# SwiGLU operands of the second half of the tokens by way of DRAM, down products kept back, and a plan with more time for low parts

## The chip, the core and the metric

The kernel runs on one core of a Trainium2 chip. The metric is the device time of one execution in microseconds (us). TensorE (PE) multiplies; its weight loads have a track of their own (PEld). VectorE (DVE), ScalarE (ACT) and GpSimd (POOL) work element by element, and the queue of SyncE (SP) issues nearly all transfers (DMA).

## The reference

One transformer block on 2048 tokens of width 512, batch 1, all float32, with a modulation that is computed from a condition vector `c`:

```python
mod = (_silu(c) @ w_mod).reshape(c.shape[0], 6, 1, -1)
sa, ca, ga, sb, cb, gb = (mod[:, 0], ..., mod[:, 5])
h = _layernorm(x, axis=-1) * (1 + ca) + sa
x = x + ga * attention(h)          # 32 heads of 16, causal window of 256, output product wo
h = _layernorm(x, axis=-1) * (1 + cb) + sb
gate = h @ w1; up = h @ w3         # 512 -> 1792 each
x = x + gb * ((_silu(gate) * up) @ w2)
```

## The kernel before

**Precision.** Every operand of a product is kept as two tiles: a high part, which is the value rounded to the type that TensorE reads at full rate, and a low part, which is the value less the high part. A product is three matmuls: high by high, high by low and low by high. The high part is made by ACT, the low part by POOL or DVE. `split` (lines 914 to 922) does both for tiles that come from DRAM.

**Stages.** Attention fills the first half of the time; its order is written by hand. Behind it come the output product with the second residual (`o_proj`, line 1068 for the matmuls), and then the feed-forward part, which the change is about. The last part of attention and all that follows are ordered by a planner, `Sched.deal`: each operation has an engine, a planned duration, a key (the smaller, the earlier it is chosen among those that can start) and the tiles that it reads and writes. It simulates the engines and writes the instructions out in the order that it finds; each engine's queue then runs in that order, and every wait is for the data itself. `CAPS` says how many PSUM banks each use may hold. The dictionary `K` holds the keys' offsets and the engines chosen for some operations; `fl` is the spacing of the keys from one block of features to the next. Keys and planned times only set an order: nothing on the chip waits for a clock.

**Feed-forward.** The tokens are worked through in two halves of 1024, and a half in seven blocks `p` of 256 features of gate and up. In a block, `ffn` makes gate and up (`up(0)`, `up(1)`) by a scheme of seven products for a two by two block matrix instead of eight. The right-hand operands are the seven operands `B11, T2, T3, T1, B21, T4, B22` (in the order of their use, each two tiles of 512 tokens for the two slices of the width, high and low), made from the four quarters of the modulated, normalised and transposed rows: width halves by token halves. T1 to T4 are differences: T1 = h12 - h11, T2 = h22 - T1, T3 = h22 - h12, T4 = h21 - T2. Each product is two slices of the width by three matmuls of 128 by 128 by 512 (line 1253). The block ends with eight down products (line 1344), six matmuls each, whose results DVE adds to the residual rows `x1` (line 1349). The downs of a block are issued during the up products of the next.

**Operands of a half.** `ln2(half)` makes the tiles of B and T: ACT normalises eight row tiles (line 1177), TensorE turns each by four transposes into a bank (line 1191), ACT modulates while copying out (line 1195), POOL and DVE take the differences (line 1208), ACT makes the high parts (line 1214) and POOL or DVE the low parts (line 1216). `ln2(0)` runs behind the output product, `ln2(1)` at the boundary of the halves. There is one set of these tiles, and two sets of weight tiles, `WT[0]` and `WT[1]`, taken in turn: block `p` of either half uses set `p % 2`, so that the last block of the first half (p = 6) and the first of the second (p = 0) use the same set. The normalised rows of `ln2` lie in eight buffers, `wqr`, `e0` to `e2` and `g0` to `g3`; the last four are also the gates of a block.

**Weights.** `load_w` loads a block's weights from DRAM (line 1126) and splits them (lines 918 and 920), `load_w2` the two rows of tiles of w2 (line 1159), for which there is one buffer. During the first half, `late_job` still prepares sums of weights for later blocks: it loads to `e0` or `e1`, works on POOL and stores (line 1156). The output goes out from line 1353.

**After the up products** of a block: gate by ACT (Silu, line 1276), times up by DVE (line 1280), high part by ACT (line 1323), low part by DVE (line 1326), and then the down products can start. The parts of all blocks lie in the same eight buffers (`wq00` to `qk2`).

Of the kernel before, what the change touches and what calls it, by code (L numbers as in the profile page):

```python
# [18 lines left out]
P = 128  # L19
# [34 lines left out]
CAPS = dict(up=3, dn=5)  # L54


def act(n):
    return 0.053 + 0.00083 * n
# [38 lines left out]
class Sched:  # L97
# [35 lines left out]
    def deal(self):  # L133
# [17 lines left out]
        while left:  # L151
# [87 lines left out]
def us(t):  # L239
# [15 lines left out]
K = dict(wo=0.254, x1=5.304, xb=-4.504, xl=0.319, os=0.261, ol=(-6.755, 2.066, 21.413, 4.993),  # L255
         pl=(9.985, -12.537, 2.397, 130.962), pe=(5.247, -7.512, 44.055, 93.798), o=(2.808, 8.131,
         12.136, 6.541), n=(3, 1, 1, 1), w0=0.022, l2=1.493, f=3.77, fl=36.492, by=((('POOL',
         'POOL'), ('POOL', 'DVE'), ('DVE', 'DVE'), ('DVE', 'DVE')), (('POOL', 'POOL'), ('DVE',
         'POOL'), ('DVE', 'POOL'), ('POOL', 'DVE')), (('POOL', 'POOL'), ('POOL', 'DVE'), ('POOL',
         'POOL'), ('DVE', 'POOL')), (('POOL', 'DVE'), ('DVE', 'DVE'), ('POOL', 'DVE'), ('POOL',  # L260
         'POOL'))), w=0.195, dn=0.541, ds=0.105, l3=-19.958)
@with_exitstack
def block_kernel(ctx: ExitStack, tc: tile.TileContext, x, wqk, wv, wo, w13, w2, c, wmod, out):
# [28 lines left out]
    wsum = drm.tile([NP, 2, 2, P, 4 * P], F32, name="wsum")  # L292

# [621 lines left out]
    def split(hi, lo, key, kh, kl, kr=None, raw=None, n=512):  # L915

        src = raw or (lambda: lo().bitcast(F32))
        sch.op("ACT", lambda: nc.scalar.activation(hi(), src(), AF.Copy), act(n), key,  # L918
               [kr or kl], [kh])
        sch.op("POOL", lambda: nc.gpsimd.tensor_tensor(out=lo(), in0=src(), in1=hi().bitcast(F32),  # L920
                                                       op=ALU.subtract), 0.06 + 0.0024 * n, key,
               [kr or kl, kh], [kl])
# [105 lines left out]
    def on_eng(e):  # L1028
        return nc.vector if e == "DVE" else nc.gpsimd

# [58 lines left out]
    def fp_open(key):  # L1089
        def go():  # L1090
# [12 lines left out]
            f"g{m}" for m in range(4)] + [f"e{m}" for m in range(3)]  # L1103
# [14 lines left out]
    def load_w(half, p, key):  # L1118
        s = p % 2
# [38 lines left out]
    def load_w2(p, key):  # L1158
        dma(lambda: nc.sync.dma_start(W2[1].bitcast(F32), w2g[p]), key,
            [("w2g", p, f) for f in range(2)], [("w2", f, 1) for f in range(2)], 512)  # L1160
# [72 lines left out]

    downs = []

    def ffn(half, p, key, fl):
        s = p % 2
        gk = {}

# [77 lines left out]
        for t in range(2):  # L1317
            for f in range(2):
                o = 2 * f + t
                hn, ln = (("wq00", "wq10"), ("wq01", "wq11"), ("qkr", "qk0"), ("qk1", "qk2"))[2 * t + f]  # L1320
# [3 lines left out]
                    fresh(hk + (0,), hn, F32R), tiles[gk[o]], AF.Copy), act(512) + 0.1,  # L1324
                       k1 + 0.5 * (2 * t + f), [f"g{o}"], [hn])
                sch.op("DVE", lambda o=o, hk=hk, ln=ln: nc.vector.tensor_tensor(  # L1326
                    out=fresh(hk + (1,), ln, F32R), in0=tiles[gk[o]],
                    in1=tiles[hk + (0,)].bitcast(F32), op=ALU.subtract), dve(512) + 0.1,
                       k1 + 0.5 * (2 * t + f), [f"g{o}", hn], [ln])

        def down():
            load_w2(p, key + fl * (K["dn"] + K["ds"] * 8))
            for t in range(2):
                for i in range(4):
                    at = 8 * half + 4 * t + i
                    bk = Bank("dn")
                    kk = key + fl * (1 + K["dn"] + K["ds"] * (4 * t + i))

                    def go(t=t, i=i, bk=bk):
                        m = 0  # L1340
                        for f in range(2):
                            hk = hs[f, t][0]
                            for h, y in PARTS:
                                nc.tensor.matmul(ps(bk), tiles[hk + (h,)][:, i * P:(i + 1) * P],  # L1344
                                                 W2[y][:, f], start=(m == 0), stop=(m == 5))
# [47 lines left out]
    for half in range(2):  # L1393
        for p in range(NP):
# [17 lines left out]
            if n:  # L1412
                add_(k - 0.05, lambda half=half, p=p, k=k: load_w(half, p, k - fl + K["w"]), ("w", n))
# [57 lines left out]
```

## Time and profile before

| | us |
|---|---|
| three runs | 1082.97, 1086.78, 1091.92; median 1086.78 |
| the profiled execution | 1086.46 |
| its span, first to last instruction | 1084.7 |
| PE busy / share of the span | 1005.1 / 93% |
| DVE / ACT / POOL busy | 728.2 / 562.9 / 587.6 |
| mean granted clock of TensorE | 0.975 |

Attention with its output product reaches to about 620 us, the first half of the feed-forward part from about 600 to 826, the second half from 850 to the end. Views that the text uses: the page, whose slices are fortieths of the span in tenths of busy time; windows, which give each engine's busy time and number of instructions in a stretch, with TensorE's granted clock (1.00 is full) and the transfers; the timeline, one row for neighbouring instructions of one kind with start, length and, in brackets, the idle time before and what ended it; groups by line, with count, total and mean; and waits, with total, number and longest. A matmul's row is longer than the time it takes from the next, because matmuls overlap; the distance between starts is what one costs.

### The profile page before, as it was taken

Reading aid. Unit: us, or ns where it says so; the run is one execution under the profiler, and the core shown is the slowest. Engines: PE = TensorE matmul, PEld = TensorE weight load, DVE = VectorE, ACT = ScalarE, POOL = GpSimd, SP = SyncE. Lnnn points to the kernel's source line nnn. Section 1 sums busy time; section 2 is a strip of 40 time slices with the busy share of each in tenths; the row PEclk is TensorE's granted clock in tenths of the full one; section 3 lists DMA queues with packets and bytes.
Section 4 is the critical chain, followed back from the end, with each engine's and each line's share of the span. In section 5 each row is a group of like instructions: output and inputs, shape, how many; then the busy total and the mean of one; then the engine's idle time right before and its main releaser. Section 6 shows DMA issues by size and latency. Waiting matters only on the chain.

```text
span 1084.7 us, 17131 instructions
## 1 busy us (share of the span) xinstructions
PE 1005.1 (93%) x5432; PEld 721.3 (66%) x5432; DVE 728.2 (67%) x1887; ACT 562.9 (52%) x1252; POOL 587.6 (54%) x727
## 2 busy tenths in 40 slices
PE   5999999999999999999897899999997999999997
PEld 3677666565656555565465677877776777778785
DVE  7685677676767676777635866566766876655665
ACT  2435667676666666667557644333535533333221
POOL 7432655665565656565548476878745444444211
PEclk9999999999999999999899999999998999999998
DMA  7621555544464545445666153655322321222002
GB/s 280 175 50 43 154 121 126 125 107 118 114 163 116 130 114 139 118 117 135 190 204 214 56 169 117 207 182 164 132 70 91 102 78 55 88 88 79 30 1 97
DMA packets 74510, 131.68 MB, mean 121 GB/s; under 512 B 8626, under 2 KB 21426, under 8 KB 74292
## 3 DMA queue, kind: packets, MB, share of 16 engines
q1 hardware_dynamic: 73700, 129.54, 42.0%
q10 hardware_dynamic: 720, 1.05, 0.3%
q8 instruction: 43, 0.70, 0.3%
q14 instruction: 47, 0.39, 0.1%
HBM read 79.96 MB, written 30.41 MB: 102 GB/s over the span
## 4 chain that ended last, share of the span: by engine, by line
PE 50%; DVE 13%; POOL 13%; DMA 12%; issue 7%; ACT 3%; SPq 1%; POOLq 0%; DVEq 0%; ACTq 0%
PE mx L1253 8%; PE st L1253 7%; DMA ring<-qk 7%; POOL qk L419 5%; PE st L1344 5%; PE mx L1344 4%; PE mx L456 4%; PE pj L401 4%; PE st L621 4%; PE po L683 4%; PE st L707 3%; PE pj L1344 3%; DVE g L1280 3%; POOL pt L735 2%; DVE wq L1326 2%
## 5 line engine op out<-in xcount | busy, mean ns | idle before, releaser
L463 DVE CUSTOM_DVE_ANT_0 junk<-mx,mskq 128x384 bf16<-128x384 f32 (+2 forms) x512 | 267.6, 528 | 89.6 <-PE mx L456 86.5
L456 PE MATMUL mx<-ring 96*128 96x384 f32 (+2 forms) x512 | 178.0, 361 | 28.5 <-DMA ring<-qk 18.9
L707 PE MATMUL st<-ring 100*128 100x384 f32 (+2 forms) x512 | 159.4, 356 | 3.1 <-ACT pt L728 2.0
L401 PE MATMUL pj<-hT,wq 128*128 128x512 f32 x384 | 155.9, 421 | 0.4 <-DVE hT L321 0.4
L456 PEld LDWEIGHTS mx<-ring 96*128 96x128 f32 x512 | 95.7, 192 | 90.5 <-DVE mt L463 40.8
L920 POOL TENSOR_TENSOR w<-w,w 128x512 fp32r<-128x512 f32 (+2 forms) x60 | 114.4, 1918 | 63.3 <-ACT w L918 63.3
L735 POOL TENSOR_SCALAR_AFFINE_SELECT pt<-pt 128x256 f32<-128x256 f32 x224 | 90.0, 406 | 82.2 <-ACT pt L728 74.4
L728 ACT ACTIVATE pt<-st 128x256 f32<-128x256 f32 x224 | 84.9, 395 | 53.7 <-DVE st L725 52.7
L683 PE MATMUL po<-pt,vS 128*17 128x384 f32 (+2 forms) x1408 | 111.8, 397 | 0.1
L707 PEld LDWEIGHTS st<-ring 100*128 100x128 f32 x512 | 98.5, 195 | 16.1 <-ACT pt L728 5.6
L419 POOL TENSOR_TENSOR qk<-qkr,qk 128x512 fp32r<-128x512 f32 x64 | 82.2, 1284 | 41.7 <-ACT qkr L407 39.2
L719 ACT ACTIVATE pt<-st 128x384 f32<-128x384 f32 (+2 forms) x172 | 77.2, 456 | 37.1 <-PE st L710 32.3
L725 DVE COPY_PREDICATED st<-later,st 128x128 f32<-128x128 uint8 x224 | 65.5, 293 | 45.6 <-PE st L707 45.3
L1296 POOL TENSOR_TENSOR t<-t,t 128x512 f32<-128x512 f32 x28 | 36.2, 1293 | 106.1 <-DVE t L1284 98.7
L401 PEld LDWEIGHTS pj<-hT,wq 128*128 128x128 f32 x384 | 73.4, 193 | 25.7 <-issue 18.4
L1253 PE MATMUL mx<-b,w 128*128 128x512 f32 x312 | 78.5, 393 | 2.6 <-ACT t L1287 2.6
L1253 PE MATMUL st<-b,w 128*128 128x512 f32 x288 | 72.1, 392 | 0.0
L1253 PEld LDWEIGHTS mx<-b,w 128*128 128x128 f32 x312 | 58.8, 189 | 15.8 <-ACT t L1287 3.0
L1276 ACT ACTIVATE g<-t 128x512 f32<-128x512 f32 x42 | 25.9, 629 | 83.2 <-POOL t L1296 60.0
L1253 PEld LDWEIGHTS st<-b,w 128*128 128x128 f32 x288 | 54.4, 189 | 11.8
L1284 DVE TENSOR_TENSOR t<-st,t 128x512 f32<-128x512 f32 x51 | 35.0, 686 | 37.2 <-PE st L1253 34.3
L1280 DVE TENSOR_TENSOR g<-t,g 128x512 f32<-128x512 f32 x42 | 56.6, 1349 | 2.9 <-POOL t L1296 1.0
(229 smaller groups left out, 2053.2 us busy)
## 6 DMA issues: line engine op xcount, KB each, us to landing
ring<-qk SPq DMA_DIRECT2D x192, 128.0 KB
o_dr<-os SPq DMA_DIRECT2D x32, 256.0 KB
w<-wsum SPq DMA_DIRECT2D x16, 512.0 KB
w<-w2g SPq DMA_DIRECT2D x14, 512.0 KB
jb<-in_w SPq DMA_DIRECT2D x24, 256.0 KB
w<-wraw SPq DMA_DIRECT2D x16, 384.0 KB
wraw<-in_w SPq DMA_DIRECT2D x7, 768.0 KB
vS<-in_wmod SPq DMA_DIRECT2D x20, 256.0 KB
```

The lines of the kernel that those rows point to most:

```text
L401: nc.tensor.matmul(v["ps"], WQ[g][w][:, n // 3], hTp(i, n // 3, b * BT, BT), start=(n == 0), stop=(n == 3 * KC - 1))
L419: nc.gpsimd.tensor_tensor(out=v[n], in0=v["raw"], in1=v[1].bitcast(F32), op=ALU.subtract)
L456: nc.tensor.matmul(v[i][:, :n], queries(NS, a, gq, 1), keys(NS, hh, a, k0, gq + 1 - k0), start=True, stop=True)
L463: nc.vector.tensor_tensor_reduce(out=junk[:, :n], in0=v[i][:, :n], in1=mskq[:, 3 * P - n:], scale=1.0, scalar=-3e38, op0=ALU.add, op1=ALU. ...
L683: nc.tensor.matmul(po[32 * i:32 * i + DH + 1, qb * P:(qb + nq) * P], vS[:, kb, 4 * g + i], pts[i // 2][:, i % 2, c0:c0 + nq], start=first, ...
L707: nc.tensor.matmul(ps[:, :nq], keys(NM, hh, a, kb, 1), queries(NM, a, kb, nq), start=True, stop=not plus)
L728: nc.scalar.activation(held[u, j, a][:, hh, :2], v[j, a, hh][:, :2], AF.Exp, scale=SCALE)
L735: nc.gpsimd.affine_select(out=pt[:, :, 2 * m], in_=pt[:, :, 0], **w)
L920: sch.op("POOL", lambda: nc.gpsimd.tensor_tensor(out=lo(), in0=src(), in1=hi().bitcast(F32), op=ALU.subtract), 0.06 + 0.0024 * n, key, [kr ...
L1253: nc.tensor.matmul(ps(bk), WT[s, n][w][:, col], BB[t, k][r], start=start and c == 0, stop=stop and c == 5, skip_group_check=True)
L1280: sch.op("DVE", lambda: nc.vector.tensor_mul(tiles[gk[o]], src(), tiles[gk[o]]), dve(512) + 0.1, k1, reads + [gn], [gn])
L1344: nc.tensor.matmul(ps(bk), tiles[hk + (h,)][:, i * P:(i + 1) * P], W2[y][:, f], start=(m == 0), stop=(m == 5))
```

## The change

- **Operands by way of DRAM.** `ln2(1)` is gone. In the first half, `half_rows` normalises, turns and modulates the rows of the second half's tokens (at blocks 1 and 2) and stores the eight tiles to `h_dr`, all by way of one tile `e3`; `half_sums` (at blocks 3 and 4) loads them again, takes the eight differences on POOL and stores them to `t_dr`. At the boundary `load_b` loads 14 tiles straight into the places of the low parts and calls `split` on each; `K["be"]` says which engine makes each low part.
- **Weight tiles** alternate across the boundary: the set is `(half * NP + p) % 2`.
- **The last blocks.** The down products of the block before the last get `K["de"]` on their key. The last block has other buffers for four of its parts, and its w2 goes to the free first tile of weight set 0.
- **The plan.** The result of ACT, DVE or POOL that TensorE reads counts as ready 0.8 us later (`PEM`); up products may hold five banks instead of three, and the transposes of `half_rows` one; the planned time of the low parts of the gated features goes to 1.0 us; all numbers in `K` are others, among them those for the last part of attention and the output product.

```diff
-CAPS = dict(up=3, dn=5)
+CAPS = dict(tp=1, up=5, dn=5)
...
             for u in o.users:
-                u.est = max(u.est, s + (o.lat if u.eng != o.eng or o.kb else o.occ))
+                m = PEM if u.eng == "PE" and o.eng in ("ACT", "DVE", "POOL") else 0.0
+                u.est = max(u.est, s + (o.lat + m if u.eng != o.eng or o.kb else o.occ))
...
+PEM = 0.8
...
-K = dict(wo=0.254, x1=5.304, xb=-4.504, xl=0.319, os=0.261, ol=(-6.755, 2.066, 21.413, 4.993),
-         pl=(9.985, -12.537, 2.397, 130.962), pe=(5.247, -7.512, 44.055, 93.798), o=(2.808, 8.131,
-         12.136, 6.541), n=(3, 1, 1, 1), w0=0.022, l2=1.493, f=3.77, fl=36.492, by=((('POOL',
...
-         'POOL'))), w=0.195, dn=0.541, ds=0.105, l3=-19.958)
+K = dict(be=(('DVE', 'POOL'), ('DVE', 'POOL'), ('DVE', 'POOL'), ('DVE', 'POOL'), ('DVE', 'POOL'),
+         ('POOL', 'POOL'), ('DVE', 'POOL')), hr=9.016, de=18.699, wo=0.403, x1=3.432, xb=-3.473,
+         xl=0.573, os=0.346, ol=(-6.127, -2.69, 14.829, 4.08), pl=(10.986, -0.476, -6.236,
+         31.344), pe=(5.042, -12.993, 12.016, 237.531), o=(3.133, 8.773, 14.919, 2.52), n=(1, 1,
+         1, 1), w0=0.71, l2=1.803, f=4.032, fl=41.71, by=((('POOL', 'POOL'), ('DVE', 'DVE'),
...
+         dn=0.504, ds=0.172, l3=-112.914)
...
+    h_dr = drm.tile([KC, 2, P, BT], F32, name="h_dr")
+    t_dr = drm.tile([4, 2, P, BT], F32, name="t_dr")
...
-        s = p % 2
+        s = (half * NP + p) % 2
...
+    def w2_of(last, part, f):
+        return WT[0, 0][part][:, f * D:f * D + D] if last else W2[part][:, f]
+
+    def w2_keys(last, f, q):
+        return [("w", 0, 0, q, s) for s in range(2)] if last else [("w2", f, q)]
+
+    def load_w2(p, last, key):
+        def go():
+            to = (WT[0, 0][1][:, :2 * D].rearrange("p (f c) -> p f c", f=2) if last else W2[1])
+            nc.sync.dma_start(to.bitcast(F32), w2g[p])
+        dma(go, key, [("w2g", p, f) for f in range(2)],
+            [y for f in range(2) for y in w2_keys(last, f, 1)][:2], 512)
         for f in range(2):
-            split(lambda f=f: W2[0][:, f], lambda f=f: W2[1][:, f], key + 4 + 1.3 * f,
-                  ("w2", f, 0), ("w2", f, 1))
+            split(lambda f=f: w2_of(last, 0, f), lambda f=f: w2_of(last, 1, f), key + 4 + 1.3 * f,
+                  w2_keys(last, f, 0), w2_keys(last, f, 1))
...
+    def half_rows(t, at_):
+
+        names = ("wqr", "e2", "t4", "t5")
+        b = 2 + t
+        ln_rstd(b, at_)
+        for i in range(4):
+            def go(i=i):
+                h = fresh(("xn", 1, 4 * t + i), names[i], F32, (P, D), "a1" if i == 0 else "fp")
+                nc.scalar.activation(h, x1(4 * b + i), AF.Identity, bias=LN[b][3][:, i:i + 1],
+                                     scale=LN[b][2][:, i:i + 1])
+            o = sch.op("ACT", go, act(512) + 0.1, at_, [("x1", 4 * b + i), "rsB%d" % b, "nbB%d" % b], [names[i]])
+            o.est = at_
+        for kk in range(4):
+            bk = Bank("tp")
+
+            def turn(kk=kk, bk=bk):
+                for i in range(4):
+                    nc.tensor.transpose(ps(bk)[:, i * P:(i + 1) * P],
+                                        tiles["xn", 1, 4 * t + i][:, kk * P:(kk + 1) * P], ident)
+
+            def mod(kk=kk, bk=bk):
+                nc.scalar.activation(fresh(("h", kk, t), "e3", F32, (P, BT), "fp"), ps(bk), AF.Identity,
+                                     bias=modc[:, 2, kk:kk + 1], scale=modc[:, 3, kk:kk + 1])
+            sch.op("PE", turn, 4 * TURN, at_, names, [bk])
+            sch.op("ACT", mod, act(512) + 0.15, at_, [bk], ["e3"])
+            dma(lambda kk=kk: nc.sync.dma_start(h_dr[kk, t], tiles["h", kk, t]), at_ + 0.5 * kk, ["e3"],
+                [("h_dr", kk, t)])
+
+    def half_sums(k, at_):
+
+        def load(kk, t, name):
+            y = ("hs", k, kk, t)
+            dma(lambda: nc.sync.dma_start(fresh(y, name, F32, (P, BT), "fp"), h_dr[kk, t]), at_,
+                [("h_dr", kk, t)], [name], hold=True)
+            return y, name
+
+        def sub(m, o, a, b):
+            sch.op("POOL", lambda: nc.gpsimd.tensor_tensor(out=tiles[o[0]], in0=tiles[a[0]], in1=tiles[b[0]],
+                                                           op=ALU.subtract), 1.29, at_, [a[1], b[1]], [o[1]])
+            dma(lambda: nc.sync.dma_start(t_dr[m - T1, k], tiles[o[0]]), at_, [o[1]], [("t_dr", m, k)])
+        h11 = load(k, 0, "t4")
+        h12 = load(k, 1, "t5")
+        h22 = load(k + 2, 1, "e2")
+        sub(T1, h11, h12, h11)
+        sub(T3, h12, h22, h12)
+        h21 = load(k + 2, 0, "e3")
+
+        sub(T2, h22, h22, h11)
+        sub(T4, h21, h21, h22)
+
+    def load_b(key):
+
+        for n, m in enumerate((B11, T2, T3, T1, B21, T4, B22)):
+            for k in range(2):
+                if m in (B11, B21, B22):
+                    src = h_dr[k if m == B11 else k + 2, 1 if m == B22 else 0]
+                    dep = ("h_dr", k if m == B11 else k + 2, 1 if m == B22 else 0)
+                else:
+                    src, dep = t_dr[m - T1, k], ("t_dr", m, k)
+                dma(lambda m=m, k=k, src=src: nc.sync.dma_start(BB[m, k][1].bitcast(F32), src),
+                    key + 0.1 * n, [dep], [("b", m, k, 1)])
+                split(lambda m=m, k=k: BB[m, k][0], lambda m=m, k=k: BB[m, k][1], key + 0.1 * n,
+                      ("b", m, k, 0), ("b", m, k, 1), eng=K["be"][n][k])
+
...
-                hn, ln = (("wq00", "wq10"), ("wq01", "wq11"), ("qkr", "qk0"), ("qk1", "qk2"))[2 * t + f]
+                hn, ln = (("wq00", "wq10"), ("wq01", "wq11"), ("qkr", "qk0"), ("qk1", "qk2"),
+                          ("e0", "e1"), ("e2", "wqr"))[2 * t + f + (2 if last and t else 0)]
                 hk = ("hh", half, p, f, t)
                 hs[f, t] = hk, hn, ln
                 sch.op("ACT", lambda o=o, hk=hk, hn=hn: nc.scalar.activation(
-                    fresh(hk + (0,), hn, F32R), tiles[gk[o]], AF.Copy), act(512) + 0.1,
+                    fresh(hk + (0,), hn, F32R, (P, BT), "fp" if hn[0] == "e" else "a1"), tiles[gk[o]], AF.Copy), act(512) + 0.1,
                        k1 + 0.5 * (2 * t + f), [f"g{o}"], [hn])
                 sch.op("DVE", lambda o=o, hk=hk, ln=ln: nc.vector.tensor_tensor(
-                    out=fresh(hk + (1,), ln, F32R), in0=tiles[gk[o]],
-                    in1=tiles[hk + (0,)].bitcast(F32), op=ALU.subtract), dve(512) + 0.1,
+                    out=fresh(hk + (1,), ln, F32R, (P, BT), "fp" if ln[0] == "e" else "a1"), in0=tiles[gk[o]],
+                    in1=tiles[hk + (0,)].bitcast(F32), op=ALU.subtract), 1.0,
...
-                    kk = key + fl * (1 + K["dn"] + K["ds"] * (4 * t + i))
+                    kk = key + fl * (1 + K["dn"] + K["ds"] * (4 * t + i)) + (
+                        K["de"] if half and p == NP - 2 else 0.0)
...
+            if half == 0 and p in (1, 2):
+                add_(k - 0.3, lambda p=p: half_rows(p - 1, te + K["hr"] + 20 * (p - 1)), ("rows", p - 1))
+            if half == 0 and p in (3, 4):
+                add_(k - 0.3, lambda p=p: half_sums(p - 3, te + K["hr"] + 40 + 15 * (p - 3)), ("sums", p - 3))
...
-                add_(k + 0.01, lambda k=k: ln2(1, k + K["l3"]), ("ln2", 1))
+                add_(k + 0.01, lambda k=k: load_b(k + K["l3"]), ("ln2", 1))
```

More of the change, by code (lines that the diff above doesn't have):

```diff
@@ L913, in fresh, with on_eng, split, src @@
         return tiles[key]
[L915 to L922, printed above, removed]
+    def on_eng(e):
+        return nc.vector if e == "DVE" else nc.gpsimd
+    def split(hi, lo, key, kh, kl, n=512, eng="POOL"):
+        def src():
+            return lo().bitcast(F32)
+        kh, kl = (y if isinstance(y, list) else [y] for y in (kh, kl))
+        sch.op("ACT", lambda: nc.scalar.activation(hi(), src(), AF.Copy), act(n), key, kl, kh)
+        sch.op(eng, lambda: on_eng(eng).tensor_tensor(
+            out=lo(), in0=src(), in1=hi().bitcast(F32), op=ALU.subtract),
+               0.06 + 0.0024 * n if eng == "POOL" else 0.85, key, kl + kh, kl)
     LN = {}
@@ L1234, in block_kernel @@
     downs = []
     def ffn(half, p, key, fl):
-        s = p % 2
+        s = (half * NP + p) % 2
         gk = {}
+        last = half == 1 and p == NP - 1
         def up(n):
```

19 lines of the change are left out of this document (7 added, 12 removed).

## The prediction

> **What bounds the kernel now.** I read the page first, for the engines and the slices, and then one view of windows for the time after attention, because every edit lies there.
>
> ```profile
> span 1084.7 us, 17131 instructions
> PE 1005.1 (93%) x5432; PEld 721.3 (66%) x5432; DVE 728.2 (67%) x1887; ACT 562.9 (52%) x1252; POOL 587.6 (54%) x727
> PE   5999999999999999999897899999997999999997
> ```
>
> TensorE bounds it. From 560 us on, the question is how far each window falls short of a TensorE that never waits and runs at full clock. The columns are window, length, PE busy (x instructions), PEld, DVE, ACT, POOL, granted clock, DMA share and GB/s.
>
> ```profile
> 560.00:600.00 40.00, 33.27 (x147) 25.57 (x145) 21.60 (x41) 27.67 (x50) 30.57 (x20) 0.96 0.63 205
> 600.00:660.00 60.00, 53.41 (x216) 41.65 (x215) 39.24 (x61) 32.16 (x56) 35.13 (x26) 0.94 0.34 111
> 660.00:820.00 160.00, 158.12 (x680) 126.95 (x679) 104.77 (x122) 62.05 (x96) 110.10 (x100) 1.00 0.44 147
> 820.00:862.00 42.00, 33.90 (x138) 26.16 (x137) 34.85 (x36) 24.50 (x39) 20.74 (x13) 0.88 0.24 81
> 862.00:1062.00 200.00, 195.70 (x842) 157.37 (x841) 123.13 (x152) 68.34 (x108) 77.34 (x44) 1.00 0.21 66
> 703.71 1.40 PE pj L1253 x6
> 596.44 0.60 PE L1191 MATMUL st<-ident,g 128*128 128x128 f32 x4
> 596.79 2.32 PE L1068 MATMUL st<-wo,o 128*128 128x512 f32 x9
> ```
>
> Six 512-wide matmuls at full clock take 1.40 us (the chain row), so one takes 0.233. Four transposes start 0.35 us ahead of what follows them (596.44 to 596.79), some 0.1 each; I take 0.11. Counted so, 660 to 820 holds 158.7 us of work in 160, and 862 to 1062 holds 196.5 in 200: almost nothing to win. From 820 to 862 there are 106 matmuls and 32 transposes, 24.7 + 3.5 = 28.2 us of work in 42: **13.8 us lost**, of which 8.1 is idle and the rest is matmuls at a lower clock. From 560 to 660, 331 matmuls and 32 transposes make 80.7 in 100: 19.3 lost. The 32 are from the code: eight turns of four for each half, and each of these windows holds one half's.
>
> The boundary between the halves, by the timeline (start, length, engine, line):
>
> ```profile
> 813.45 1.53 PE L1253 MATMUL st<-b,w 128*128 128x512 f32 x6
> 820.35 0.33 SPq L1159 DMA_DIRECT2D w<-w2g  x1
> 824.39 0.36 SPq L1126 DMA_DIRECT2D w<-wraw  x1
> 824.53 0.61 ACT L918 ACTIVATE w<-w 128x512 fp32r<-128x512 f32 x1
> 824.79 1.64 PE L1253 MATMUL st<-b,w 128*128 128x512 f32 x6
> 836.30 1.52 ACT L1177 ACTIVATE g<-x1b,nbB,rsB 128x512 f32<-128x512 f32 x2 [3.24 <-DVE qk L1326]
> 837.17 0.44 PE L1191 MATMUL st<-ident,g 128*128 128x128 f32 x2 [2.52 <-ACT g L1177]
> 850.73 1.53 PE L1253 MATMUL mx<-b,w 128*128 128x512 f32 x6
> 854.82 2.36 PE L1253 MATMUL mx<-b,w 128*128 128x512 f32 x6 [2.56 <-ACT t L1287]
> ```
>
> The first half's last up product is 824.79 to 826.4 and the second half's first one starts at 850.73. The normalised rows wait for the buffers g0 to g3, which the last low parts of the first half still read until 836.3; only then follow transposes, modulation, differences and parts. TensorE has only down products to bridge this.
>
> The end of the kernel:
>
> ```profile
> 1057.90 0.33 SPq L1159 DMA_DIRECT2D w<-w2g  x1
> 1061.98 1.53 PE L1253 MATMUL mx<-b,w 128*128 128x512 f32 x6
> 1062.78 2.95 POOL L920 TENSOR_TENSOR w<-w,w 128x512 fp32r<-128x512 f32 x2 [1.18 <-ACT w L918]
> 1066.33 0.98 PE L1344 MATMUL mx<-w,wq 128*128 128x512 f32 x3 [1.72 <-DVE wq L1326]
> 1068.85 5.29 PE L1344 MATMUL st<-w,wq 128*128 128x512 f32 x12
> 1080.03 1.10 PE L1344 MATMUL mx<-w,qk 128*128 128x512 f32 x4
> ```
>
> After the last up product (1063.4, by its own pipelined end) TensorE has only the last eight down products, 48 matmuls, 11.2 us at full clock. They end at 1081.1, so 17.7 us pass: **6.5 us lost**, in waits for the chain gate, high part, low part, and then in twelve matmuls that take 5.29 us instead of 2.8.
>
> **The boundary term.** What the change moves from here is the normalising, turning and modulating; the differences are made on POOL in the first half. What stays is 14 loads from DRAM and 14 pairs of high and low parts. The groups of 820 to 862 give the durations (count, busy us, mean ns):
>
> ```profile
> L1216 DVE TENSOR_TENSOR b<-t,b 128x512 fp32r<-128x512 f32 x10 | 8.6, 884 | 3.8 <-ACT b L1214 3.7
> L1208 DVE TENSOR_TENSOR t<-t,t 128x512 f32<-128x512 f32 x6 | 8.4, 1394 | 0.1
> L1214 ACT ACTIVATE b<-t 128x512 fp32r<-128x512 f32 x14 | 8.3, 625 | 6.3 <-DVE t L1208 6.2
> L1216 POOL TENSOR_TENSOR b<-t,b 128x512 fp32r<-128x512 f32 x4 | 6.4, 1632 | 0.6 <-ACT b L1214 0.6
> L1208 POOL TENSOR_TENSOR t<-t,t 128x512 f32<-128x512 f32 x2 | 2.8, 1379 | 6.8 <-ACT t L1195 6.8
> L1177 ACT ACTIVATE g<-x1b,nbB,rsB 128x512 f32<-128x512 f32 x4 | 3.1, 810 | 4.3 <-DVE qk L1326 3.2 <-DVE wq L1326 1.0
> L1195 ACT ACTIVATE t<-mx,modc 128x512 f32<-128x512 f32 x3 | 2.3, 773 | 0.0
> ```
>
> An operand tile is free when its last product of the first half has read it. Seven groups of six before the end that is B11's, which I take to be the one at 813.45; it ends by 815. The 512 KB load of w2 issued at 820.35 was being converted at 824.53, 4.2 us later, and a 256 KB load should not take longer. High part 0.63, low part on POOL 1.63: B11 is ready at about 815 + 4.2 + 2.3 = 821.5, before the first half's last product. B22, the last, is free at 826.4 and ready at 832.9, while its product is seventh, at 826.4 + 6 x 1.40 = 834.8 at the earliest, and eight down products (11.2 us) lie in between. The 14 loads are 3.7 MB in some 15 us, 245 GB/s, beside the 81 GB/s of that window. POOL needs 8 x 1.63 = 13 us for low parts instead of 6.4 + 2.8, DVE sheds six differences (8.4 us) and four low parts. The set of weight tiles also alternates across the boundary now, so the load that could go out only at 824.39 goes out about one block of features earlier. Work on the path is then only TensorE's own. I take 12.5 of 13.8, leaving a stop of an ordinary block; bounds 0 and 13.8.
>
> **What the first half pays.** Added there: 8 normalisings and 8 modulations on ACT, 8 x 0.81 + 8 x 0.77 = 12.6 us; 32 transposes, 3.5 us, already counted as work in the 28.2; 8 differences on POOL, about 8 x 1.38 = 11 us; 8 stores of rows, 8 loads, 8 stores of differences, 24 issues on SP. ACT is idle 27.8 us of 600 to 660, where x1 of the second half becomes ready, and POOL 49.9 of 660 to 820. That idle time is the cover; without it the ACT term is 12.6 and the POOL term 11. I take +2 in all, nearer to nothing because both engines are idle for longer than the work they get; bounds 0 and 23.6.
>
> The Trainium skill speaks against this step: "GPSIMD Engine Reference", section 8 (Key points), says that GpSimd shares its SBUF interfaces with VectorE and that they contend when the VectorE instruction has two SBUF inputs. The profile's L1208 on DVE, two SBUF inputs, has a mean of 1394 ns. By that rule VectorE loses as much time as the moved differences last, and the sum would be 9 us worse if all of it reached TensorE; the rival further down prices it from the rows.
>
> **The tail.** The down products of the block before the last get 18.7 us on their due time, so some of them run after the last up products; the last block has buffers of its own for its parts and its w2 goes to a free weight tile, so its load need not wait as the one at 1057.90 did and POOL's 2.95 us at 1062.78 leave the path. Counted from the key of the block before the last, with a spacing of 41.7 and 0.63 of it for a block, the last up product stands at 41.7 + 26.3/2 + 6 x 26.3/14 = 66.1, and the kept-back downs at 26.3 x 1.504 + 18.7 = 58.3 and every 4.5 after: six of them come later, 6 x 1.40 = 8.4 us, and the gap from 1063.4 to 1068.85 is 5.4. It is covered. I take 6.0 of 6.5; bounds 0 (if the planner runs them early where TensorE would stall) and 6.5.
>
> **The steady blocks.** More time for low parts (0.8 us planned on each result that TensorE takes from another engine) and five banks instead of three let up products run ahead. What is there to win:
>
> ```profile
> PE pj L1344 <- DVE wq L1326: 3.5, 4, 1.1
> PE st L1344 <- DVE t L1284: 0.8, 1, 0.8
> SPq L1156 <- POOL e L834: 64.6, 15, 20.3
> ```
>
> The first two are all of TensorE's waits from 862 to 1062, 4.3 us; I take 1.5 of them, bounds -2 and 4.3. The third row is of SP's own waits from 560 on.
>
> **The replanned joint of attention and feed-forward.** All due times of 560 to 660 change at once. Nothing in the trace says which way; 0, bounds half of the 19.3 lost either way, 9.7 less to 9.7 more.
>
> **The sum.** -12.5 + 2 - 6.0 - 1.5 + 0 = -18.0. The profiled execution took 1086.46 us beside a span of 1084.7, and the runs shown have a median of 1086.78, so the two agree within 0.4: 1086.5 - 18.0 = 1068.5.
>
> **Rivals.**
>
> *Half the boundary.* POOL becomes the bound there: in the block of features around it (132 matmuls, 30.8 us), 13 us of operand parts, the next weights' low parts (one at 1632 or longer for each 512 columns; 7 of them per block, 11.4), w2's pair 2.95 and two gate sums make some 30. For it: the means already stretched; against it: POOL was busy for half of the window. If half of the boundary and half of the tail come back late, the gain is 6.3 + 3 - 2 = 7: 1079.5.
>
> *VectorE held by POOL's differences.* L1208 on DVE has a mean of 1394 ns where L1216, of the same size, has 884: DVE is slow while POOL works. If the 11 us of differences reach TensorE through DVE instead of the 2 taken: 1077.5. Against it: DVE was idle for 55 us of 660 to 820.
>
> *The early joint gains too.* If the longer planned times recover half of the 19.3: 1058.8. For it: waits of TensorE on parts there; against it: the ACT work added in that very window.
>
> *Slower: ACT stands behind one staging tile.* All eight modulated row tiles pass through one buffer, e3; the next modulation waits until the store before it has landed, and on ACT every gate and high part queues behind it; TensorE waits for those. A store waits at SP too: 64.6/15 = 4.3 us each in the row of L1156, and lands some 4.2 later. Six such waits, 8.5 each, are 51 us of ACT; less its 27.8 idle, 23 remain. At the boundary 8.1 us idle came with 5.7 of low clock, so 23 idle cost 39: 1107.5. It decides once a wait is over 4.6 us (27.8/6). Against it: the plan orders other ACT work between two modulations where it expects the store to be late.
>
> *The down products are not kept back.* A key is an order, not a hold. Then the tail keeps 6: 1074.5, inside the forecast's own spread.
>
> **How the numbers follow.** A chance of 0.46 for the forecast, with the unkept tail as part of it (1062 to 1075.5); 0.14 for the early joint (1054 to 1062); 0.16 for half the boundary (1076 to 1092); 0.06 for VectorE held (1076 to 1080); 0.18 for the staging tile. About 1%, 11 us, is what a measurement of this kernel can tell from no change. Faster by more than that: 0.46 + 0.14 = 0.60; within it 0.16 + 0.06 = 0.22; slower 0.18. The range, 1056 to 1092, leaves out the staging tile and the edge of the early joint, 0.2.
>
> **What would show it.** Right: 820 to 862 with TensorE over 41 us busy and clock 1.00; no normalising and no transposes at the boundary; down products of the block before the last right behind the last up product, and no matmul at half clock from there on. Wrong: ACT waiting for DMA at the new modulation, TensorE waiting for parts of b after the boundary, or windows 600 to 820 longer than 220 us for the same products.

## The result

| | before | changed |
|---|---|---|
| runs shown | 1082.97 to 1091.92 | 1053.03 to 1062.59 |
| median, us | 1087.57 (4 runs) | 1055.47 (4 runs) |
| the profiled execution, us | 1086.46 | 1062.59 |
| ratio, 95% interval | | 0.9707 [0.9650, 0.9765] |

The kernel is 2.9% faster, 32 us; the forecast was 18, and the median lies half a microsecond under the forecast range. The same kernel once more gave 1054.80 against 1090.50, ratio 0.9687 [0.9644, 0.9730].

The page of the changed kernel, as before: span, engines, TensorE's slices.

```profile
span 1060.9 us, 17248 instructions
PE 999.1 (94%) x5432; PEld 719.3 (68%) x5432; DVE 698.8 (66%) x1878; ACT 564.7 (53%) x1252; POOL 595.2 (56%) x736
PE   5999999999999999999788999999999999999998
```

The dip behind the middle (the joint of attention and feed-forward) is still there; the dip of the boundary is gone, and the last slice, cut by the end of the span, is nearly full. The windows, with the same columns as before:

```profile
560.00:600.00 40.00, 35.43 (x158) 25.84 (x157) 22.62 (x43) 21.57 (x43) 23.20 (x16) 0.91 0.69 230
600.00:660.00 60.00, 56.45 (x254) 44.26 (x252) 43.97 (x68) 45.23 (x79) 40.14 (x31) 0.97 0.35 125
660.00:820.00 160.00, 159.88 (x699) 129.49 (x698) 102.03 (x125) 68.54 (x106) 123.86 (x113) 1.00 0.58 194
820.00:862.00 42.00, 41.38 (x178) 33.16 (x177) 33.16 (x40) 18.98 (x32) 25.74 (x16) 1.00 0.51 169
862.00:1037.00 175.00, 175.00 (x758) 142.01 (x758) 96.53 (x138) 66.54 (x103) 72.97 (x44) 1.00 0.22 69
```

From 820 to 862 TensorE is busy for 41.38 us at clock 1.00, where it was 33.90 at 0.88, and from 862 to the last up product it never stops. ACT has 45.23 busy from 600 to 660 where it had 32.16: there stand the new normalisings and modulations.

The boundary, by the timeline:

```profile
810.95 1.01 SPq L1314 DMA_DIRECT2D b<-h_dr  x2
823.94 4.25 PE L1339 MATMUL mx<-b,w 128*128 128x512 f32 x18
827.75 0.89 SPq L1314 DMA_DIRECT2D b<-h_dr  x2
828.03 0.62 PE L1432 MATMUL pj<-w,qkr 128*128 128x512 f32 x2
829.24 6.37 POOL L932 TENSOR_TENSOR b<-b,b 128x512 fp32r<-128x512 f32 x4 [2.41 <-ACT b L931]
830.82 2.96 PE L1339 MATMUL st<-b,wo 128*128 128x512 f32 x12
833.62 2.96 PE L1339 MATMUL mx<-b,wo 128*128 128x512 f32 x12
838.60 1.67 PE L1339 MATMUL mx<-b,wo 128*128 128x512 f32 x6 [0.62 <-ACT t L1377]
```

The first loads of operands go out at 810.95, while the first half's up products still run; the last go out at 827.75, right when its last up product is through (the 18 matmuls from 823.94). Two down products of the block before follow at 828.03, and the second half's first up product starts at 830.82, 3.0 us after the last matmul of the first half's up products began instead of 24.7. One wait of 0.62 us is all that is left, and the eight down products of the first half's last block are not needed as a bridge: they run later, from 848.5 on.

The end:

```profile
1015.04 0.32 SPq L1178 DMA_DIRECT2D w<-w2g  x1
1036.04 1.56 PE L1339 MATMUL mx<-b,o 128*128 128x512 f32 x6
1037.44 1.56 PE L1432 MATMUL mx<-w,wq 128*128 128x512 f32 x6
1045.84 2.96 PE L1432 MATMUL mx<-w,wq 128*128 128x512 f32 x12
1056.74 0.39 PE L1432 MATMUL mx<-w,wqr 128*128 128x512 f32 x1
```

Six kept-back down products fill 1037.44 to 1045.84, and the last eight follow at 1.40 us each, none at half clock. The last w2 was loaded at 1015.04, 21 us ahead of the last up product.

**A ledger at equal work.** The two profiled executions differ by 23.8 us in span, the medians by 32. Most of the difference between the two figures is attention: its 28th store (of 32), ahead of which the two kernels have the same order, lies at 505.26 in the profile of before and at 511.77 in that of the change, but at 504.14 in the second profile of the change and at 507.06 in the second of before. So the profiles are compared from that store on, at equal work of TensorE: each 512-wide matmul of output product, up and down counts 0.233 us and each transpose 0.109, and a mark is the moment when so much is done. The table gives the time between marks, worked out from the matmul starts of the traces.

| stretch (work, us) | before | before again | changed | again | the changed plan's difference |
|---|---|---|---|---|---|
| joint: 28th store to 80 | 146.0 | 148.6 | 143.8 | 142.4 | -4.2 |
| first half: 80 to 240 | 162.0 | 162.1 | 159.1 | 159.1 | -2.9 |
| boundary: 240 to 290 | 64.1 | 64.6 | 50.8 | 50.8 | -13.5 |
| second half: 290 to 462 | 176.5 | 176.5 | 170.6 | 170.6 | -5.9 |
| end: 462 to the last instruction | 31.0 | 30.9 | 24.8 | 24.8 | -6.1 |

The differences are between the means of two profiles; their sum is -32.6, and the medians differ by 32.1. Behind the joint the stretches repeat to 0.1 us, at the boundary of before to 0.5; the joint moves by up to 5 us from execution to execution. Seven profiles of this and the next section have TensorE's order in the joint exactly as in the changed kernel; they lie between 142.4 and 147.3, with a mean of 145.0, 2.3 less than the mean of the two of before. That is less than before's own two differ, so a gain at the joint is not clear of its movement.

### The profile page after: what moved, and what is told of

It reads as the page before. It is cut to its first block, busy times and chain, and to the rows that moved or that the text cites. A ratio compares the mean times of both kernels' runs of the same rounds, so it can differ in the third digit from the quotient of the medians.

```text
span 1060.9 us, 17248 instructions
## 1 busy us (share of the span) xinstructions
PE 999.1 (94%) x5432; PEld 719.3 (68%) x5432; DVE 698.8 (66%) x1878; ACT 564.7 (53%) x1252; POOL 595.2 (56%) x736
## 4 chain that ended last, share of the span: by engine, by line
PE 62%; DMA 12%; POOL 10%; DVE 7%; issue 4%; ACT 3%; SPq 1%; POOLq 0%; ACTq 0%; DVEq 0%
PE st L1339 11%; PE mx L1339 10%; DMA ring<-qk 8%; PE mx L1432 6%; PE st L1432 6%; PE mx L464 5%; PE pj L409 5%; POOL qk L427 4%; PE po L691 4%; PE st L629 4%; PE st L715 4%; PE pj L1432 3%; PE pj L1339 2%; POOL pt L743 2%; DMA o_dr<-os 2%
## 5 line engine op out<-in xcount | busy, mean ns | idle before, releaser
L715 PE MATMUL st<-ring 100*128 100x384 f32 (+2 forms) x512 | 161.4, 359 | 2.7 <-ACT pt L736 1.9
L409 PE MATMUL pj<-hT,wq 128*128 128x512 f32 x384 | 158.2, 428 | 1.5 <-DVE hT L329 1.2
L932 POOL TENSOR_TENSOR w<-w,w 128x512 fp32r<-128x512 f32 (+2 forms) x56 | 98.7, 1769 | 54.9 <-ACT w L931 52.6
L736 ACT ACTIVATE pt<-st 128x256 f32<-128x256 f32 x224 | 85.1, 394 | 54.5 <-DVE st L733 53.3
L1370 DVE TENSOR_TENSOR t<-mx,t 128x512 f32<-128x512 f32 x51 | 35.1, 689 | 54.6 <-PE mx L1339 44.7
L1410 ACT ACTIVATE wq<-g 128x512 fp32r<-128x512 f32 x28 | 17.8, 634 | 93.2 <-DVE g L1366 64.2
L1339 PE MATMUL st<-b,w 128*128 128x512 f32 x264 | 65.9, 392 | 0.6 <-DVE b L1236 0.6
L1339 PE MATMUL mx<-b,w 128*128 128x512 f32 x258 | 64.1, 393 | 0.4 <-DVE b L1236 0.4
L1339 PEld LDWEIGHTS st<-b,w 128*128 128x128 f32 x264 | 49.2, 188 | 11.5 <-DVE b L1236 1.1
L1339 PEld LDWEIGHTS mx<-b,w 128*128 128x128 f32 x258 | 49.0, 190 | 11.4 <-DVE b L1236 0.9
```

What stands on the lines that cost most here:

```text
L409: nc.tensor.matmul(v["ps"], WQ[g][w][:, n // 3], hTp(i, n // 3, b * BT, BT), start=(n == 0), stop=(n == 3 * KC - 1))
L715: nc.tensor.matmul(ps[:, :nq], keys(NM, hh, a, kb, 1), queries(NM, a, kb, nq), start=True, stop=not plus)
L736: nc.scalar.activation(held[u, j, a][:, hh, :2], v[j, a, hh][:, :2], AF.Exp, scale=SCALE)
L932: sch.op(eng, lambda: on_eng(eng).tensor_tensor(out=lo(), in0=src(), in1=hi().bitcast(F32), op=ALU.subtract), 0.06 + 0.0024 * n if eng == ...
L1339: nc.tensor.matmul(ps(bk), WT[s, n][w][:, col], BB[t, k][r], start=start and c == 0, stop=stop and c == 5, skip_group_check=True)
```

## The experiments

All are compared stretch by stretch with the changed kernel, unless they start from the one before; the medians stand beside that, and they carry the 5 us of the joint and the several of attention.

**The changed kernel again.**

> The changed kernel as it is, to see which part of the difference between the two profiled executions belongs to the execution. Theory: attention up to the 28th store of its result is the same code, and its 6.5 us more in the profiled execution of the changed kernel (505.3 against 511.8 us) is chance of that execution; here the 28th store lies at 505 to 508 and the time at 1053 to 1056. Rival: the two new DRAM tensors move the others and slow attention; the store stays at 511 or later.

The 28th store is at 504.14, a little earlier still than the theory had it, and the profiled execution took 1053.58. In all 18 profiles every engine has the same instructions in the same order up to this store, and it lies between 500.81 and 511.77. The offset was chance, and the ledger above follows. The kernel before, profiled once more, took 1091.45 us; its stretches are the ledger's second column.

**Operands made at the boundary again.**

```diff
-            if half == 0 and p in (1, 2):
+            if False:
                 add_(k - 0.3, lambda p=p: half_rows(p - 1, te + K["hr"] + 20 * (p - 1)), ("rows", p - 1))
-            if half == 0 and p in (3, 4):
+            if False:
                 add_(k - 0.3, lambda p=p: half_sums(p - 3, te + K["hr"] + 40 + 15 * (p - 3)), ("sums", p - 3))
...
-                add_(k + 0.01, lambda k=k: load_b(k + K["l3"]), ("ln2", 1))
+                add_(k + 0.01, lambda k=k: ln2(1, k - 19.958), ("ln2", 1))
```

> The changed kernel with the operands of the second half made at the boundary again (ln2(1) in place of half_rows, half_sums and load_b); weight tiles still alternate, everything else as changed. Theory: the 13.3 us that the boundary gained at equal work come from the operands, so 10 to 14 us are lost there, 1066 to 1069; the first half, freed of 16 ACT and 8 POOL operations, gains at most 1. Rival: the alternating weight tiles, which let the weights of the next block load early, carry it; then at most 4 are lost, 1056 to 1060.

1071.77 us. The boundary is 62.5, 11.7 longer; the stretch ahead of it (165 to 240) 2.6 longer; from 80 to 165, freed of the new work, 0.4 shorter. TensorE's waits from 805 to 860 are the old kind, for the normalised rows and for the first products' banks, and its granted clock from 810 to 852 is 0.88, as it was at the boundary before.

```profile
PE mx L1211 <- ACT g L1197: 4.2, 1, 4.2
PE st L1339 <- ACT t L1373: 3.4, 1, 3.4
```

**Weight tiles as before.** The set is `p % 2` again, the last w2 in set 1.

> The changed kernel with the weight tiles as before, so that the last block of the first half and the first of the second use the same set (the last block's w2 then goes to the other set). Theory: with the operands ready early the weights become what the boundary waits for, since their load can go out only when the last products have read the old ones, and 4 to 8 us are lost there. Rival: the eight held down products cover the load and the parts as they did before; at most 2 are lost.

1056.05 us. The boundary is 50.5, no longer than with alternating tiles. The rival held: the weights were not what the boundary waited for, neither with the old operands (11.7 of the 13.5 us come back in `ln2_back` although the tiles alternate there) nor with the new.

**The end without its three parts, and with one or two of them.** `no_keep` has de 0, the eight buffers for every block and w2 in its one tile; `no_keep_key` has only de 0; `w2_only` has only w2's free tile of the three, `buffers_only` only the four other buffers.

```diff
-... hr=9.016, de=18.699, ...
+... hr=9.016, de=0.0, ...
-        last = half == 1 and p == NP - 1
+        last = False
```

> The changed kernel without its end: no kept-back down products, the last block in the same eight buffers and its w2 in the one w2 tile. Theory: the end loses its 6.3 us, TensorE waits after the last up product and comes back at half clock: 1060.5 to 1063. Rival: five banks and the longer planned times already bring down products behind the last up product, so at most 2 are lost.

> The changed kernel with the added due time of the down products of the block before the last set to nothing (de 0); the last block keeps its own buffers and the free tile for w2. The run without both lost 8.0 us at the end. Theory: the kept-back downs are what fills TensorE there, so 4 to 7 come back: 1059 to 1062. Rival: buffers and w2 carry it, since the low parts could start earlier and without POOL beside them; at most 2 come back.

> The changed kernel with the free weight tile for the last w2 alone: no added due time for the downs, and the last block's parts in the same eight buffers as every block's. Theory: in the run without all three TensorE waited 3.9 us for w2's high part at the end, since w2's load went out only when the downs of the block before had read the one w2 tile; the free tile alone therefore keeps the end at 24.8 to 26 us from 462 us of work on. Rival: the parts in buffers of their own are needed too; the end is 28 or more.

> The changed kernel with buffers of their own for the last block's parts alone: no added due time, and the last w2 in the one w2 tile. Theory (w2's place): the end is as without all three, 31 to 33 us from 462 us of work on. Rival (buffers): it stays at 25 to 27.

| | due time kept | own buffers | w2 in a free tile | end, us | median, us |
|---|---|---|---|---|---|
| changed | yes | yes | yes | 24.8 | 1055.47 |
| no_keep_key | no | yes | yes | 25.2 | 1057.39 |
| w2_only | no | no | yes | 24.9 | 1054.58 |
| buffers_only | no | yes | no | 33.1 | 1062.81 |
| no_keep | no | no | no | 32.8 | 1068.74 |

Without all three the end lost 8.0 us, more than I had forecast. With w2 in the free tile it takes 24.8 to 25.2 us, whatever the other two are, and without it 32.8 to 33.1: w2's place carries the gain, and the other two are not needed beside it. The added due time without the free tile was not run, so it is not shown that it could not have covered the gap by itself; the down products that it keeps back read the one w2 tile, though, so that the load would have to wait for them. The timeline of `no_keep` at its end shows what happens without:

```profile
1042.98 0.32 SPq L1178 DMA_DIRECT2D w<-w2g  x1
1046.39 1.15 ACT L931 ACTIVATE w<-w 128x512 fp32r<-128x512 f32 x2 [2.30 <-DMA w<-w2g]
1047.07 0.63 PE L1431 MATMUL mx<-w,wq 128*128 128x512 f32 x1 [3.94 <-ACT w L931]
1048.42 2.50 PE L1431 MATMUL mx<-w,wq 128*128 128x512 f32 x5 [0.72 <-POOL w L932]
1050.72 2.76 PE L1431 MATMUL pj<-w,wq 128*128 128x512 f32 x6
```

The load of w2 goes out when the downs of the block before have read the one tile; 4.1 us later TensorE has its high part, and what follows runs at half clock for a while (six matmuls in 2.56 us, 1050.72 to 1053.28, at a granted clock of 0.50). With w2 in place already, the plan leaves two down products behind the last up product even without the added due time, and these 2.8 us are enough.

**The plan: margin, banks, pace.** `no_margin` plans with PEM 0 and the low parts as before; `caps3` gives up products three banks; `pace_back` takes the old fl, w, dn and ds; `plan_back` joins the first and the third; `before_margin` and `before_pace` add margin or pace alone to the kernel before.

> The changed kernel with no margin in the plan: PEM 0 and the low parts of the gated features planned as before. Theory: the 4.3 us of TensorE's waits for parts between 862 and 1062 and those of the first half come back, 5 to 9 us in all over the steady blocks, 1060 to 1064. Rival: the five banks and the new pace of the keys took these waits away; the time stays within 2 us of the changed kernel's.

> The changed kernel with three banks for up products instead of five. The run without the margin left the steady blocks of the second half as short as the changed kernel's, so the margin is not what took 5.9 us there (3.7 + 2.2 at equal work). Theory now: with five banks the last up products of a block no longer wait for a bank, the chain to the parts starts earlier, and this is the 5.9; here 5 to 7 us come back over the second half and 2 to 3 in the first, 1062 to 1066. Rival: the new spacing and due times of the down products (fl, dn, ds) do it, by leaving downs to cover the chain; then the second half stays within 1 us and the time within 1053 to 1058.

> The changed kernel with the old spacing of the keys and the old due times of weights and down products (fl 36.492, w 0.195, dn 0.541, ds 0.105). Theory (five banks): the second half stays within 1 us at equal work between 290 and 462 us of it. Rival (the pace): 5 to 7 us come back there. The end may lose up to 6 in either case, because the key of the kept-back downs is counted in this spacing.

> The changed kernel with neither the margin nor the new pace (PEM 0, low parts planned as before, fl 36.492, w 0.195, dn 0.541, ds 0.105). Each alone left the second half's steady blocks untouched. Theory: they stand in for one another, since both put the down products later than the parts that they need; with both undone the 5.9 us of work 290 to 462 come back, beside some 3 us at 165 to 240, 4 to 6 at the boundary and 5 in the joint: 1070 to 1076. Rival: what took the waits away is something else of the change (operands that are ready early, another set of weight tiles); the second half then stays within 1 us and the time is 1063 to 1068.

> The kernel before with the margin alone (0.8 us on what TensorE reads from ACT, DVE or POOL, low parts of the gated features planned with 1.0 us). Theory: the margin by itself is enough for the second half, 5 to 6 us less at 290 to 462, and takes 3 to 5 from the joint; boundary and end stay as before: 1075 to 1080. Rival: the margin works only together with the new due times; at most 2 us less.

> The kernel before with the new pace alone (fl 41.71, w -0.242, dn 0.504, ds 0.172). Theory: the pace by itself is enough too, 5 to 6 us less at 290 to 462 and some 3 less at 165 to 240; joint, boundary and end within 2 us of before: 1076 to 1081. Rival: at most 2 us less, and the two are not interchangeable.

| | joint | 80 to 240 | boundary | 290 to 462 | end | median, us |
|---|---|---|---|---|---|---|
| before (two profiles) | 147.3 | 162.0 | 64.3 | 176.5 | 31.0 | 1087.57 |
| changed (two profiles) | 143.1 | 159.1 | 50.8 | 170.6 | 24.8 | 1055.47 |
| no_margin | 150.8 | 158.6 | 54.7 | 170.6 | 24.8 | 1063.81 |
| caps3 | 145.9 | 158.6 | 51.7 | 170.6 | 24.8 | 1057.82 |
| pace_back | 143.7 | 161.4 | 53.3 | 170.6 | 24.8 | 1060.23 |
| plan_back | 151.3 | 161.9 | 51.5 | 176.3 | 24.8 | 1072.50 |
| before_margin | 145.8 | 161.4 | 63.3 | 170.8 | 30.9 | 1076.33 |
| before_pace | 151.6 | 162.6 | 61.2 | 170.7 | 31.5 | 1082.28 |

Two of my theories fell in turn: neither the margin alone nor the banks took the second half's waits away (the time without the margin came out in the stated range, but through the joint and the boundary). The third held both ways: margin and pace stand in for one another. Either alone, in either kernel, brings the second half to 170.6 to 170.8; with both undone it is 176.3 again, and TensorE's waits from 860 to 1040 are those of before, under other line numbers (down products for the low part of a gated feature):

```profile
PE mx L1424 <- DVE wq L1405: 4.2, 5, 1.1
```

In the changed kernel the view of waits from 820 to 1040 has one row, the 0.6 us at the boundary. Beside the second half `before_pace` did not go as expected: its joint is 4.3 us longer and its boundary 3.1 shorter, where I expected both within 2. At the boundary the plan has a part of its own that is not understood: with the new operands 3.9 us are lost without the margin and 2.5 with the old pace, but only 0.7 with both undone. What is called the margin here is two edits, `PEM` and the planned time of the low parts; they were not taken apart.

**The joint.** `joint_back` has the old numbers for the last part of attention, the output product and the first operands; `margin2` has PEM 1.6.

> The changed kernel with the old numbers for the last part of attention, the output product and the first operands (wo, x1, xb, xl, os, ol, pl, pe, o, n, by, l2, w0, f). Theory: these numbers took the 5.4 us that the joint gained at 3 to 80 us of work (1.9 + 3.5) and cost the 1.5 to 3.2 ahead of it, so the joint is 2 to 4 us longer here, 1057 to 1060. Rival: the margin does it, since the run without it lost 5.5 there; then the old numbers with the margin stay within 2.

> The changed kernel with twice the margin, PEM 1.6. Theory: the steady blocks have no waits left, so they stay as they are; only the joint (3 to 45 us of work), where the margin of 0.8 was worth 5.5, can gain, 0 to 3: 1052 to 1056. Rival: more margin leaves TensorE with nothing planned to do at the joint and the boundary and the time rises to 1058 or more.

The joint took 146.8 with the old numbers (1060.53 us) and 150.6 with the double margin (1063.34 us), against 145.0 for the changed plan (142.4 to 147.3) and 150.8 with no margin. So the old numbers cannot be told from the new ones by this stretch, though the median is 5 us higher. More margin is not better: 0 and 1.6 both cost some 6 us against 0.8, one profile each and medians 8 us higher, and the rival's time came about, though at the joint and not at the boundary (49.9). TensorE's largest waits of the joint with the double margin are for a low part of the output product's operand and for a bank:

```profile
PE st L1077 <- POOL x1b L1060: 3.5, 1, 3.5
PE pj L1339 <- ACT t L1373: 3.0, 1, 3.0
```

The first of them is there with 0.8 too (3.1 us in the first profile). Why 0.8 suits the joint better than 0 or 1.6 was not settled; its numbers differ with every plan, and the runs do not show a cause beyond that.

**A simpler version.** With w2's free tile alone at the end, the kernel is as fast (1054.58, ratio to before 0.9699 [0.9657, 0.9741]) with less in it.

## Why the prediction was right or wrong

The forecast's terms add to 18 us and the measured ones to 32.6. The boundary and the end, 18.5 of the sum, came out at 19.6. The step that failed is the other three terms: the first half at +2, the steady blocks at -1.5 and the joint at 0, together +0.5, came out at -13.0. I held that TensorE had almost nothing to win in the steady stretches; the runs show that it lost 5.6 us there in the second half and 3.0 in the first, and that the new plan took nearly all of it.

- **Second half's steady blocks: mis-sized by 4.4 us.** -1.5 forecast, -5.9 measured. I took a third of the 4.3 us of waits that the trace showed, without a row that said why the rest should stay; all of them went, by the margin or by the pace, either of which is enough. The stops were also longer than their rows: a row counts from a matmul's modelled end, 0.39 us after its start, where the next could have started 0.23 after it, and the first matmul behind each stop took 0.34. From start to start the five stops of the kernel before between 862 and 1062 cost 5.6 us. My count of the work hid this, because I took 0.233 us for each matmul from one row: 300 of the 840 there have their weights in the tile w and take 0.227 (below), so the window had lost some 2 us more than the 3.5 that I counted.
- **First half: wrong sign, off by 4.9 us.** +2 forecast, -2.9 measured. From 80 to 165, where the new work stands, the stretch is 84.9 in both kernels. It is 0.4 shorter in the run without the new work, but also in five runs that keep it, so a price of the new work is not to be seen. At 165 to 240, 2.8 us went away. The same unit price had made 660 to 820 look full: by the distance between starts its stops cost 3.0 us in the kernel before. These are its waits there, and the changed kernel's view from 660 to 820 has none:

```profile
PE mx L1344 <- POOL w L920: 1.1, 2, 0.9
PE st L1344 <- DVE wq L1326: 0.8, 1, 0.8
```

  The gain goes away with the old pace and with the old operands, each alone, but through other waits (in `ln2_back` a single one of 2.3 us, for a result of DVE), so it has no single cause that the runs show.
- **Joint: 0 forecast**, -4.2 in the two profiles that are counted above, -2.3 over seven. Without the margin the joint took 150.8 to 151.6 wherever another new number was in the plan (`no_margin`, `plan_back`, `before_pace`); with 0.8 us of it the joint took 142.4 to 147.3 in every profile, against 146.0 to 148.6 for the kernel before. The margin is therefore worth some 6 us beside the other new numbers; by itself in the kernel before it shows 1.5 (`before_margin`), less than that kernel's two profiles differ, and that the new numbers alone bring anything is not shown.
- **Boundary: right.** -12.5 forecast, -13.5 measured, and 11.7 of it by the operands, as said. The stations were near too: loads from 810.95 on (I had 815), the eight low parts on POOL with a mean of 1.65 us (1.63), one wait of 0.62 us. The half sentence on the alternating weight tiles was wrong as a cause: taken away, they cost nothing.
- **End: right in size by luck, wrong in its main cause.** -6.0 forecast, -6.1 measured. I named the kept-back down products as the cover and w2's place as an addition. Beside w2's free tile the due time is worth 0.4 us, and the free tile is worth 8 in the changed plan; the rival that saw the tail's 6 us lost if those products are not kept back falls with it. I read the gap at 1063 to 1069 as one that needs 5.4 us of other work; with w2 in place 2.8 us cover it. How much of the gap of the kernel before was w2's is not shown, since the free tile was not tried there: by its trace TensorE waited at the end 2.7 us for low parts from DVE and 0.4 for w2's from POOL, and two of DVE's operations beside POOL's 2.95 us took 1.65 and 1.75 us where their kind takes 0.69 elsewhere in this stretch.
- **The rivals.** ACT behind one staging tile: the groups of the modulations from 600 to 720 have one wait of 0.8 us for a store.

```profile
L1276 ACT ACTIVATE e<-mx,modc 128x512 f32<-128x512 f32 x4 | 3.1, 766 | 0.0
L1276 ACT ACTIVATE e<-st,modc 128x512 f32<-128x512 f32 x3 | 2.3, 770 | 0.8 <-DMA h_dr<-e 0.8
L1276 ACT ACTIVATE e<-pj,modc 128x512 f32<-128x512 f32 x1 | 0.8, 765 | 0.0
```

  POOL as the bound at the boundary: four of its low parts, 6.37 us in a row, ran beside products that did not wait. VectorE held by POOL's differences: the first half got shorter. The contention that the Trainium skill's "GPSIMD Engine Reference" (section 8, Key points) names is in this trace as before (a DVE low part of 1.78 us at 825.59, beside POOL's at 825.28, and one of 0.68 at 828.49 with POOL idle), but from 660 us on the view of waits has one row for TensorE, and that one is for ACT. The early joint came nearest with its 1058.8, but by luck: the joint did not give the 9.7 us on which it rests.

## What to carry to other kernels

A wait that the trace shows on the bounding engine is worth its full length until a row says why it should stay, and a planner's margin can take it away without touching the work. Before a gap is filled with other work, look for the transfer that makes it: here a load that had to wait for a buffer's last reader cost 8 us, and beside a free buffer the work kept back for the gap was worth 0.4. And where two edits can each take a wait away, undoing one shows nothing; undo both, and do each alone. Idle rows are also not the whole price of a stop: count from start to start, with the price of that very kind of matmul.

## What the runs showed of the hardware that I had not expected

- The matmuls of up products are not all equally long at full clock. In the boundary's rows above, 18 with weights in the tile w take 4.09 us from 823.94 to the next start at 828.03, 0.227 each; 12 with weights in the tile wo take 2.80 (830.82 to 833.62), 0.233. The groups of 862 to 1037 say the same in their means:

```profile
L1339 PE MATMUL mx<-b,w 128*128 128x512 f32 x120 | 29.3, 390 | 0.0
L1339 PE MATMUL mx<-b,wo 128*128 128x512 f32 x60 | 15.0, 396 | 0.0
```

  Both move the same shapes; what makes the difference was not tried.
- The same instructions of attention took 500.8 to 511.8 us up to the 28th store, over 18 profiles, while the steady blocks of a kernel repeated to 0.01 us. An edit behind attention is better judged at equal work from there than by the span.
